# Half of the small transfers from GpSimd, two preparation steps in one slot, and a ring of seven `c` tiles in a three-network kernel on one core

## The chip, the cores and the metric

The kernel runs on one core of a Trainium2 chip. The metric is the device time of one execution in microseconds (us). The engines are TensorE (PE: matmuls, with PEld its weight loads), VectorE (DVE), ScalarE (ACT), GpSimd (POOL), and SyncE (SP), which here only issues transfers.

## The reference

Three computations in a row, all in float32:

- Linear attention with decay, for 4 batches, 8 heads, 768 positions and head size 48. For every position, `state = alpha * state + k v^T` and `y = q state`. The outputs of the heads side by side are x, 3072 tokens by 384.
- A network on x: `h = x @ w_in` (384 to 2048), ELU of h, times `w_out` (2048 to 384).
- Four experts on that result: for each expert, `relu(x @ w1) @ w2` (384 to 1024 to 384), and the sum of the four weighted by the token's probabilities, which are divided by their sum first.

## The kernel before

Every float32 operand of a matmul is split into a high part and a low part, and each product is three matmuls: high by high, high by low, low by high. So each matrix that one engine makes for PE needs a pass for the high part (mostly ACT) and one for the low part (DVE or POOL).

**Network 1** runs over 96 items: 6 chunks of 512 tokens by 16 blocks of the hidden size. An item has two halves: nine matmuls of the first layer (L618) into a bank of PSUM, and nine of the second layer (L643), which take the block of two items ago. The first items are written out by hand. From item 5 on (L1185) a table `slots` (L1059 to L1071) says which step of the attention runs in which half item: a chunk is four units (one batch, 128 positions each), and the four units of the next chunk are spread over the items of the present one. A unit has the steps prep1 (L409), prep2 (L425), scores (L431), the output (`yout_t`, L471) with the state (L513), and `xtrans` (L534), which splits the output into the two parts that network 1 reads. Work that waits for another engine is put into a queue (`later`, L130) and issued at the next `flush`.

The output of a unit is copied from PSUM to the tile `yt` by ACT (L499). Six small transfers within SBUF (L505), 16 partitions by 128 elements each, then put its heads into place; SP issues all six. `xtrans` reads `yt`: ACT makes the high part (L545), DVE the low part (L546).

**Network 2** (from 502 us) has 33 iterations: 3 groups of 1024 tokens (r) by 11 blocks of hidden units (q). The products of the first layer are not taken block by block, but by a scheme with fewer matrix products: an iteration has 15 steps, each one product of three matmuls (L922) into one of two banks h0 and h1, and DVE (L936, L938, L942; POOL where no bank takes part) adds and subtracts the results into tiles `u` and, when a hidden block is complete, into a tile `c`. Each `c` then goes through `relu` (L895): ACT writes the high part (L897) and the ReLU in place (L898), POOL the low part (L900). The second layer of the iteration before (L969) is spread between the steps. When an expert ends, six products with the probabilities are taken by DVE (`gate`, L988), each into a `c` tile as well, and added to the sum by POOL (L991), at the very end by DVE.

The inputs of the first layer are sums of blocks of x. For the groups r = 1 and 2, `prep_x` (L805) makes them during q = 1 to 8 of the group before, two in an iteration, 15 in all: POOL adds (L829), ACT makes the high part (L837) and POOL the low part (L834) of a tile `xh`, which SP sends to DRAM. The `xh` tiles come from the pool tag "g", which has three buffers.

Where a `c` lies is decided by a counter in `ctile` (L842), the number of the tile modulo 5: one buffer of the tag U6, twice the tag "e" (two buffers), once "wr", once the tag "g" of `xh`. A tile from a tag takes the buffer that comes free first in the program's order, and its first writer waits until the last reader of what lay there is done.

[...]

Of the kernel before, what the change touches and what calls it, by code (L numbers as in the profile page):

```python
# [8 lines left out]
F32 = mybir.dt.float32  # L9
# [6 lines left out]
ALU = mybir.AluOpType  # L16
AX = mybir.AxisListType

B, H, S, D = 4, 8, 768, 48
# [17 lines left out]
LISTED = 5  # L37
# [3 lines left out]
NPR = NCH // 2  # L41
NG = 11
# [26 lines left out]
STEPS2 = (  # L69
    STEPS[:7] + ((6, STEPS[7][1][::2]), STEPS[8], (3, (("+", (0, 2), "b", "S2"),)), STEPS[14])  # L70
)
# [31 lines left out]
class _Fast:  # L103
# [367 lines left out]
    def yout_t(self, u):  # L471


        nc = self.nc
        c, b = u
        raw = self.raw[u]
        ps = [self.abank(), self.abank()]

        def to(h, n):
            r, c0 = 64 * (swap(h) % 2), h // 4 * C  # L480
            return ps[h // 2 % 2][r:r + n, c0:c0 + C]

        for h in range(H):
            a, r = h // 2, slice(64 * (h % 2), 64 * (h % 2) + D)
            nc.tensor.matmul(  # L485
                to(h, 64), self.st[b][r, a, :], raw[r, Q0 + a * C:Q0 + (a + 1) * C],
                start=(a < 2), stop=False, skip_group_check=True,
            )
        for h in range(H):
            nc.tensor.matmul(  # L490
                to(h, D), raw[:, V0 + h * D:V0 + (h + 1) * D],
                self.sm[u, h % 2][:, h // 2, :], start=False, stop=True, skip_group_check=True,
            )
        del self.sm[u, 0], self.sm[u, 1]

        def pack():
            y = self.ap.tile([128, NP * C], F32, tag="y", name="yt")
            for n in range(2):
                nc.scalar.copy(  # L499
                    y[0:SW].rearrange("p (a w t) -> p w a t", w=2, t=C)[:, n],  # L500
                    ps[n][0:SW, 0:2 * C].rearrange("p (a t) -> p a t", t=C),
                )
            for j in range(2):
                for k in range(KD):
                    nc.sync.dma_start(  # L505
                        out=y[64 * j + D:64 * j + 64, k * C:(k + 1) * C],
                        in_=y[64 * j + 16 * k:64 * j + 16 * k + 16, DM:NP * C],
                    )
            self.y[u] = y[:, 0:DM].rearrange("p (k t) -> p k t", k=KD)

        self.later(pack)
# [19 lines left out]

        self.later(decay)

    def xtrans(self, u):  # L534
        nc = self.nc
        c, b = u
        v = self.y.pop(u)
        if c not in self.x0:
            self.x0[c] = self.big.tile([128, 2, KD, 512], F32R, tag=f"X{c % 2}", name=f"x0_{c % 2}")
        x0 = self.x0[c]  # L540
        self.split(x0[:, 0, :, b * C:(b + 1) * C], x0[:, 1, :, b * C:(b + 1) * C], v)

    def split(self, hi, lo, src, eng=None):
        nc = self.nc
# [296 lines left out]

    def ctile(self):  # L842
        self.cn += 1
        i = self.cn % 5
        if i == 4:
            return self.uslot(6, "c")
        if i % 2:
            return self.ep.tile([128, 512], F32, tag="e", name="c")
        if i:
            return self.wp.tile([128, 3, DM], F32, tag="wr", name="c").rearrange("p n d -> p (n d)")[:, 0:512]  # L850
        return self.hp.tile([128, 2, 512], F32, tag="g", name="c")[:, 0]

# [39 lines left out]
                )  # L892
            self.pb[r, e, m] = t

    def relu(self, g, n, v):  # L895
        nc = self.nc
        nc.scalar.activation(out=g[:, n, 0], in_=v, func=AF.Relu)  # L897
        nc.scalar.activation(out=v, in_=v, func=AF.Relu)  # L898
        self.later(
            lambda: nc.gpsimd.tensor_tensor(out=g[:, n, 1], in0=v, in1=g[:, n, 0].bitcast(F32), op=ALU.subtract)  # L900
        )

    def layer1(self, i, extra):

        nc = self.nc
        r, q = divmod(i, NG)
        wa = self.wa[i]
        S, G = {}, {}
# [4 lines left out]
        for n, (p, ops) in enumerate(STEPS if q < NG - 1 else STEPS2):  # L913
# [9 lines left out]
            for op, dst, a0, a1 in ops:  # L923
                if isinstance(dst, tuple):
                    m, f = dst
# [4 lines left out]
                    out = self.ctile()  # L930
                else:
                    if dst not in S:
                        S[dst] = self.uslot(int(dst[1]), "u")
                    out = S[dst]
                if op == "=":
                    nc.vector.tensor_copy(out, b)  # L936
                elif op == "n":
                    nc.vector.scalar_tensor_tensor(  # L938
                        out=out, in0=val(a0, b), scalar=-1.0, in1=val(a1, b), op0=ALU.mult, op1=ALU.subtract
                    )  # L940
                else:
                    (nc.vector if "b" in (a0, a1) or dst == "S5" else nc.gpsimd).tensor_tensor(  # L942
                        out=out, in0=val(a0, b), in1=val(a1, b), op=ALU.add if op == "+" else ALU.subtract
                    )
                if isinstance(dst, tuple):
                    self.relu(G[m], f, out)
            extra(n)
        return G

# [67 lines left out]
    def run(self):  # L1017
# [40 lines left out]
        slots = {}  # L1058
        for c in range(1, NCH):  # L1059
            steps = [s for u in units[4 * c:4 * c + 4] for s in seq[units.index(u)]]  # L1060
            end = F1 * c
            av = half(end - F1, end - 3)
            if c == 1:
                av = half(LISTED, end - 1)
                steps[0:5] = [steps[2]]
            for n, s in enumerate(steps):
                k = av[n * len(av) // len(steps)]
                slots.setdefault(k, []).append(s)
                if n % 6 == (1 if c == 1 else 5) and (c, n) != (1, 1):
                    slots[k].append([(load_next, ())])  # L1070
            slots.setdefault((end - 1 if c == 1 else end - 2, c != 1), []).append([(self.xtrans, ((c, B - 1),))])  # L1071

        def open_p2():
            self.attn.__exit__(None, None, None)
# [400 lines left out]
```

## Time and profile before

| | us |
|---|---|
| median of 3 runs (1238.07 to 1242.77) | 1238.5 |
| profiled execution | 1237.87 |
| its span | 1236.1 |
| PE busy | 1219.7 (99%) |
| DVE busy | 868.1 (70%) |
| ACT busy | 589.5 (48%) |
| POOL busy | 490.9 (40%) |

The span is the time from the first to the last instruction of one profiled execution; 1.8 us of that execution lie around it. Busy shares are means over stages with different loads. In the timeline a row is one instruction, or several of one line in a row (x3), and the brackets give the engine's idle time before it and who ended it. A row of PEld is the load of a matmul's weights; where PE stands, it is nearly always the load that waits, and its row names what for.

### The profile page before, as it was taken

To read this page: it belongs to the slowest core of one execution; us is meant where nothing else is said; L and a number is where in the kernel's file an instruction comes from. 1 tells how busy PE (TensorE), PEld (TensorE's weight loads), DVE (VectorE), ACT (ScalarE), POOL (GpSimd) and SP (SyncE) were. 2 spreads that over 40 slices of the span, in tenths; PEclk is the share of its full clock that TensorE was granted. 3 is DMA by queue.
4 is the path that set the end of the run, shared out by engine and by line. 5 is a ranking of instruction groups with operands and counts; after the bars stand their busy time and mean duration, and the time that the engine had idled before them with its cause. 6 is when DMAs were issued, how large, how long until landed. Compare 5 with 4: busy or idle time off the path is not lost.

```text
span 1236.1 us, 17787 instructions
## 1 busy us (share of the span) xinstructions
PE 1219.7 (99%) x6469; PEld 993.6 (80%) x6469; DVE 868.1 (70%) x1433; ACT 589.5 (48%) x1092; POOL 490.9 (40%) x388
## 2 busy tenths in 40 slices
PE   8999999999999999999999999999999999999997
PEld 5787888888887888788888887888888878888886
DVE  9995877777777678657576757675766566667664
ACT  6885566666666566434334332433433233342231
POOL 2000000000000000387688847857977474456662
PEclk9999999999999999999999999999999999999999
DMA  9632554555546467536555577763656864344331
GB/s 377 218 107 89 184 182 180 184 188 200 183 164 212 144 217 266 189 141 230 192 191 208 214 289 277 256 219 143 229 192 228 326 235 169 120 159 165 107 134 57
DMA packets 64815, 239.92 MB, mean 194 GB/s; under 512 B 7640, under 2 KB 33464, under 8 KB 55376
## 3 DMA queue, kind: packets, MB, share of 16 engines
q1 hardware_dynamic: 63856, 233.99, 53.1%
q10 hardware_dynamic: 864, 4.72, 1.0%
q8 instruction: 53, 0.87, 0.3%
q14 instruction: 42, 0.34, 0.1%
HBM read 178.27 MB, written 59.42 MB: 192 GB/s over the span
## 4 chain that ended last, share of the span: by engine, by line
PE 91%; DVE 4%; POOL 1%; issue 1%; ACT 1%; DMA 0%; SPq 0%; ACTq 0%; DVEq 0%; POOLq 0%
PE h L922 25%; PE t L643 15%; PE h L618 15%; PE t L969 15%; PE a L969 11%; PE h L969 5%; PE a L439 2%; PE a L490 2%; PE a L485 1%; PE h L460 1%; PE h L521 1%; POOL acc L991 0%; DVE s_s L263 0%; DMA raw<-in_att_dram 0%; POOL c L942 0%
## 5 line engine op out<-in xcount | busy, mean ns | idle before, releaser
L900 POOL TENSOR_TENSOR g_W<-c,g_W 128x512 fp32r<-128x512 f32 x128 | 164.7, 1297 | 627.3 <-ACT c L898 599.0
L942 DVE TENSOR_TENSOR u<-h,u 128x512 f32<-128x512 f32 x258 | 177.5, 688 | 85.9 <-PE h L922 84.6
L922 PE MATMUL h<-xc_Q,wa 128*128 128x512 f32 x780 | 218.9, 390 | 0.2 <-DVE u L942 0.2
L618 PE MATMUL h<-x,w_W 128*128 128x512 f32 x864 | 214.3, 392 | 2.5 <-DVE x L546 1.3
L643 PE MATMUL t<-g,w_W 128*128 128x512 f32 x864 | 215.4, 393 | 0.0
L897 ACT ACTIVATE g_W<-c 128x512 fp32r<-128x512 f32 x128 | 80.3, 627 | 269.7 <-DVE c L942 155.9
L618 PEld LDWEIGHTS h<-x,w_W 128*128 128x128 f32 x864 | 160.5, 188 | 37.5 <-DVE x L546 1.7
L643 PEld LDWEIGHTS t<-g,w_W 128*128 128x128 f32 x864 | 160.3, 188 | 33.9 <-issue 0.4
L922 PEld LDWEIGHTS h<-xc_Q,wa 128*128 128x128 f32 x780 | 145.9, 188 | 32.1 <-DVE u L942 1.7
L969 PE MATMUL t<-g_W,wb 128*128 128x512 f32 x576 | 157.6, 389 | 0.0
L969 PEld LDWEIGHTS t<-g_W,wb 128*128 128x128 f32 x576 | 108.1, 188 | 22.5
L898 ACT ACTIVATE c<-c 128x512 f32<-128x512 f32 x192 | 121.5, 633 | 7.4
L942 DVE TENSOR_TENSOR c<-u,h 128x512 f32<-128x512 f32 x123 | 84.3, 686 | 48.9 <-PE h L922 43.3
L629 DVE SCALAR_TENSOR_TENSOR h<-e,h 128x512 f32<-128x512 f32 x96 | 66.6, 693 | 71.8 <-ACT e L628 71.5
L922 PE MATMUL h<-xc_W,wa 128*128 128x512 f32 x390 | 109.7, 390 | 2.2 <-DVE u L942 2.2
L900 POOL TENSOR_TENSOR g_X<-c,g_X 128x512 fp32r<-128x512 f32 x64 | 82.1, 1295 | 68.0 <-ACT c L898 64.8
L936 DVE COPY u<-h 128x512 f32<-128x512 f32 x99 | 68.0, 690 | 58.0 <-PE h L922 57.7
L969 PE MATMUL a<-g_W,wb 128*128 128x512 f32 x384 | 108.2, 389 | 0.0
L897 ACT ACTIVATE g_X<-c 128x512 fp32r<-128x512 f32 x64 | 40.1, 627 | 131.5 <-DVE c L942 72.9
L922 PEld LDWEIGHTS h<-xc_W,wa 128*128 128x128 f32 x390 | 73.0, 188 | 18.2 <-DVE u L942 3.2
L627 ACT ACTIVATE e<-h 128x512 f32<-128x512 f32 x96 | 57.1, 595 | 57.8 <-PE h L618 56.4
L969 PEld LDWEIGHTS a<-g_W,wb 128*128 128x128 f32 x384 | 72.1, 188 | 15.0
(163 smaller groups left out, 1790.2 us busy)
## 6 DMA issues: line engine op xcount, KB each, us to landing
wa<-wad SPq DMA_DIRECT2D x33, 1536.0 KB, 6.6
wb<-wbd SPq DMA_DIRECT2D x30, 1536.0 KB, 7.3
raw<-in_att_dram SPq DMA_DIRECT2D x22, 964.0 KB, 5.9
wad<-wh SPq DMA_DIRECT2D x44, 384.0 KB, 2.9
wbd<-wh SPq DMA_DIRECT2D x43, 384.0 KB, 3.4
xcd<-xh SPq DMA_DIRECT2D x30, 512.0 KB, 3.5
wraw<-in_we_dram SPq DMA_DIRECT2D x20, 576.0 KB, 4.8
xc_Q<-xcd SPq DMA_DIRECT2D x6, 1536.0 KB, 7.7
```

The lines of the kernel that those rows point to most:

```text
L439: nc.tensor.matmul(ps[j][:, a * C:(a + 1) * C], raw[r, K0 + a * C:K0 + (a + 1) * C], raw[r, Q0 + a * C:Q0 + (a + 1) * C], start=True, stop ...
L618: nc.tensor.matmul(h[:, 0:n], w[:, wl, fi, k * 128:(k + 1) * 128], x[:, xl, k, n0:n0 + n], start=((k, wl, xl) == TERMS[0]), stop=((k, wl, ...
L627: nc.scalar.activation(out=e, in_=h, func=AF.Relu, scale=-1.0)
L629: return lambda: nc.vector.scalar_tensor_tensor(out=h, in0=e, scalar=-1.0, in1=h, op0=ALU.add, op1=ALU.max)
L643: nc.tensor.matmul(self.xa[k][:, 0:n], w[:, wl, fi, DM + k * 128:DM + (k + 1) * 128], g[:, gl, 0:n], start=(first and i == 0), stop=(last ...
L897: nc.scalar.activation(out=g[:, n, 0], in_=v, func=AF.Relu)
L898: nc.scalar.activation(out=v, in_=v, func=AF.Relu)
L900: lambda: nc.gpsimd.tensor_tensor(out=g[:, n, 1], in0=v, in1=g[:, n, 0].bitcast(F32), op=ALU.subtract)
L922: nc.tensor.matmul(b, w[:, wl], x[:, xl], start=(j == 0), stop=(j == 2))
L936: nc.vector.tensor_copy(out, b)
L942: (nc.vector if "b" in (a0, a1) or dst == "S5" else nc.gpsimd).tensor_tensor(out=out, in0=val(a0, b), in1=val(a1, b), op=ALU.add if op == ...
L969: nc.tensor.matmul(oa[m, d], wt[:, f, wl, d * 128:(d + 1) * 128], G[m][:, f, gl], start=first, stop=last)
```

## The change

It has four parts.

- In `pack` the transfers of the second half of the heads (j = 1) are issued by POOL; SP issues the other three.
- In chunk 1's table, prep1 and prep2 of its first prepared unit are put into one slot, so there are 19 slots where 20 were, over one half item less. The steps behind it stand earlier by up to a half item. The last `xtrans` of the chunk stays where it is, but issues its low part at once and not at the next `flush`.
- The ring of `c` tiles has seven places: U6 at remainder 3, "e" at 0 and 2, "wr" at 1, and the tag "g" at 4, 5 and 6.
- In the last iteration of network 2 the last two low parts of `relu` are computed by DVE in place of POOL.

```diff
--- before.py
+++ after.py
@@ -502,7 +502,7 @@
                 )
             for j in range(2):
                 for k in range(KD):
-                    nc.sync.dma_start(
+                    (nc.sync, nc.gpsimd)[j].dma_start(
                         out=y[64 * j + D:64 * j + 64, k * C:(k + 1) * C],
                         in_=y[64 * j + 16 * k:64 * j + 16 * k + 16, DM:NP * C],
                     )
@@ -531,7 +531,7 @@
 
         self.later(decay)
 
-    def xtrans(self, u):
+    def xtrans(self, u, now=False):
         nc = self.nc
         c, b = u
         v = self.y.pop(u)
@@ -539,6 +539,8 @@
             self.x0[c] = self.big.tile([128, 2, KD, 512], F32R, tag=f"X{c % 2}", name=f"x0_{c % 2}")
         x0 = self.x0[c]
         self.split(x0[:, 0, :, b * C:(b + 1) * C], x0[:, 1, :, b * C:(b + 1) * C], v)
+        if now:
+            self.queue.pop()()
 
     def split(self, hi, lo, src, eng=None):
         nc = self.nc
@@ -841,12 +843,12 @@
 
     def ctile(self):
         self.cn += 1
-        i = self.cn % 5
-        if i == 4:
+        i = self.cn % 7
+        if i == 3:
             return self.uslot(6, "c")
-        if i % 2:
+        if i in (0, 2):
             return self.ep.tile([128, 512], F32, tag="e", name="c")
-        if i:
+        if i == 1:
             return self.wp.tile([128, 3, DM], F32, tag="wr", name="c").rearrange("p n d -> p (n d)")[:, 0:512]
         return self.hp.tile([128, 2, 512], F32, tag="g", name="c")[:, 0]
 
@@ -892,12 +894,12 @@
                 )
             self.pb[r, e, m] = t
 
-    def relu(self, g, n, v):
+    def relu(self, g, n, v, eng):
         nc = self.nc
         nc.scalar.activation(out=g[:, n, 0], in_=v, func=AF.Relu)
         nc.scalar.activation(out=v, in_=v, func=AF.Relu)
         self.later(
-            lambda: nc.gpsimd.tensor_tensor(out=g[:, n, 1], in0=v, in1=g[:, n, 0].bitcast(F32), op=ALU.subtract)
+            lambda: eng.tensor_tensor(out=g[:, n, 1], in0=v, in1=g[:, n, 0].bitcast(F32), op=ALU.subtract)
         )
 
     def layer1(self, i, extra):
@@ -943,7 +945,7 @@
                         out=out, in0=val(a0, b), in1=val(a1, b), op=ALU.add if op == "+" else ALU.subtract
                     )
                 if isinstance(dst, tuple):
-                    self.relu(G[m], f, out)
+                    self.relu(G[m], f, out, nc.vector if i == NPR * NG - 1 and n >= len(STEPS2) - 2 else nc.gpsimd)
             extra(n)
         return G
 
@@ -1061,14 +1063,14 @@
             end = F1 * c
             av = half(end - F1, end - 3)
             if c == 1:
-                av = half(LISTED, end - 1)
-                steps[0:5] = [steps[2]]
+                av = half(LISTED, end - 1)[:-1]
+                steps[0:6] = [steps[2] + steps[5]]
             for n, s in enumerate(steps):
                 k = av[n * len(av) // len(steps)]
                 slots.setdefault(k, []).append(s)
-                if n % 6 == (1 if c == 1 else 5) and (c, n) != (1, 1):
+                if n % 6 == (0 if c == 1 else 5) and (c, n) != (1, 0):
                     slots[k].append([(load_next, ())])
-            slots.setdefault((end - 1 if c == 1 else end - 2, c != 1), []).append([(self.xtrans, ((c, B - 1),))])
+            slots.setdefault((end - 1 if c == 1 else end - 2, c != 1), []).append([(self.xtrans, ((c, B - 1), c == 1))])
 
         def open_p2():
             self.attn.__exit__(None, None, None)
```

Line numbers from L541 on are higher by two in the changed kernel. How the instructions of DVE move is seen at three places.

The first is the end of chunk 0, on DVE. L629 and L635 (L631 and L637 after) belong to the ELU of an item, L429 to a unit's prep2, and L546 (L548 after) is the low part of the last output of the chunk, which is read from `yt`. Before:

```order
L429 TENSOR_TENSOR raw<-raw,P 128x512
L635 TENSOR_TENSOR g<-h_1164,g 128x512
L629 SCALAR_TENSOR_TENSOR h_1237<-e,h_1237 128x512
L546 TENSOR_TENSOR x_1_821<-yt,x_1_821 128x3x128
L635 TENSOR_TENSOR g<-h_1237,g 128x512
L629 SCALAR_TENSOR_TENSOR h_1265<-e,h_1265 128x512
L447 TENSOR_TENSOR sm<-a_1276,mask 128x512
```

and after:

```order
L429 TENSOR_TENSOR raw<-raw,P 128x512
L637 TENSOR_TENSOR g<-h_1131,g 128x512
L631 SCALAR_TENSOR_TENSOR h_1192<-e,h_1192 128x512
L637 TENSOR_TENSOR g<-h_1192,g 128x512
L548 TENSOR_TENSOR x_1_806<-yt,x_1_806 128x3x128
L631 SCALAR_TENSOR_TENSOR h_1237<-e,h_1237 128x512
L637 TENSOR_TENSOR g<-h_1237,g 128x512
```

The low part of the output has moved ahead of the ELU's step for the block h_1237; before, it stood behind it.

The second is in network 2, on DVE, where the trace of before stands at 648 to 651 us; the number behind a name tells tiles of one name apart, and the brackets hold the engines and transfers whose semaphores the instruction waits for. Before:

```order
L942 TENSOR_TENSOR c_6466<-u_6337,h1_6460 128x512 [waits DVE_49,Pool_49]
L942 TENSOR_TENSOR c_6479<-u_6406,h0_6475 128x512 [waits DVE_49,PE_49,Pool_49]
L942 TENSOR_TENSOR u_6320<-h0_6475,u_6320 128x512 [waits Pool_49]
L942 TENSOR_TENSOR c_6494<-u_6320,h1_6490 128x512 [waits DVE_49,PE_49]
L936 COPY u_6513<-h0_6509 128x512 [waits PE_49,Pool_49]
```

and after:

```order
L944 TENSOR_TENSOR c_6466<-u_6337,h1_6460 128x512 [waits DVE_49,Pool_49]
L944 TENSOR_TENSOR c_6479<-u_6406,h0_6475 128x512 [waits DMAHW1_49,DVE_49,DMAHW5_49,PE_49,Activation_49]
L944 TENSOR_TENSOR u_6320<-h0_6475,u_6320 128x512 [waits Pool_49]
L944 TENSOR_TENSOR c_6494<-u_6320,h1_6490 128x512 [waits DVE_49,PE_49,Pool_49]
L938 COPY u_6513<-h0_6509 128x512 [waits PE_49]
```

The order is the same, but the write of c_6494 now waits for POOL too: its buffer is that of c_6466, two `c` tiles before it, which POOL's L902 reads.

The third is the end of the program, on DVE: the last two `c` tiles of network 2, and the first products with the probabilities. Before:

```order
L942 TENSOR_TENSOR u<-h_11150,u 128x512
L942 TENSOR_TENSOR c<-h_11165,u 128x512
L942 TENSOR_TENSOR c<-u,h_11179 128x512
L988 TENSOR_TENSOR c<-a_9432,pb 128x512
L991 TENSOR_TENSOR acc<-acc,c 128x512
L988 TENSOR_TENSOR c<-a_9433,pb 128x512
L991 TENSOR_TENSOR acc<-acc,c 128x512
L988 TENSOR_TENSOR c<-h_9434,pb 128x512
```

and after:

```order
L944 TENSOR_TENSOR u<-h_11150,u 128x512
L944 TENSOR_TENSOR c<-h_11165,u 128x512
L902 TENSOR_TENSOR g_W_11169<-c,g_W_11169 128x512
L944 TENSOR_TENSOR c<-u,h_11179 128x512
L902 TENSOR_TENSOR g_W_11169<-c,g_W_11169 128x512
L990 TENSOR_TENSOR c<-a_9432,pb 128x512
L993 TENSOR_TENSOR acc<-acc,c 128x512
L990 TENSOR_TENSOR c<-a_9433,pb 128x512
L993 TENSOR_TENSOR acc<-acc,c 128x512
L990 TENSOR_TENSOR c<-h_9434,pb 128x512
```

Each of the last two `c` is now followed on DVE by its low part (L902), so the second `c` and the first product stand behind a low part that needs ACT's result.

## Rows read from the trace of the kernel before

**Rows 1.** The page, part 1: busy us (share of span) xinstructions.
```profile
PE 1219.7 (99%) x6469; PEld 993.6 (80%) x6469; DVE 868.1 (70%) x1433; ACT 589.5 (48%) x1092; POOL 490.9 (40%) x388
```

**Rows 2.** Waits of PE's weight loads: line, releaser: us, times, longest.
```profile
PEld h L922 <- DVE u L942: 4.9, 9, 1.5
```

**Rows 3.** Timeline, 104 to 113 us: start, duration, engine, line [idle before <-releaser].
```profile
104.75 3.67 SPq L505 DMA_DIRECT2D yt<-yt  x6
...
109.64 0.51 ACT L545 CAST x<-yt 128x384 fp32r<-128x384 f32 x1 [4.27 <-DMA yt<-yt]
...
111.95 0.55 DVE L546 TENSOR_TENSOR x<-yt,x 128x384 fp32r<-128x384 f32 x1
...
112.56 1.69 PEld L618 LDWEIGHTS h<-x,w_W 128*128 128x128 f32 x8 [1.70 <-DVE x L546]
```

**Rows 4.** Timeline, 57 to 59 us, DVE and PE.
```profile
57.24 0.69 DVE L419 SCALAR_TENSOR_TENSOR raw<-nt,raw 128x512 f32<-128x512 f32 x1
...
58.08 2.20 PE L618 MATMUL h<-x,w_W 128*128 128x512 f32 x9
```

**Rows 5.** View of the tile yt, its DMAs.
```profile
DMA to landing us min/median/max: 1.7/2.1/7.3
```

**Rows 6.** Timeline, 755 us, DVE.
```profile
755.52 0.69 DVE L942 TENSOR_TENSOR c<-u,h 128x512 f32<-128x512 f32 x1 [1.22 <-POOL g_X L900]
```

**Rows 7.** Timeline, 649 to 651 us, DVE, PEld and POOL.
```profile
649.26 0.69 DVE L942 TENSOR_TENSOR c<-u,h 128x512 f32<-128x512 f32 x1 [0.47 <-PE h L922]
...
650.88 0.64 PEld L922 LDWEIGHTS h<-xc_Q,wa 128*128 128x128 f32 x3
...
650.95 2.55 POOL L900 TENSOR_TENSOR g_X<-c,g_X 128x512 fp32r<-128x512 f32 x2
```

**Rows 8.** Timeline, 691 to 694 us, DVE, PEld and POOL.
```profile
691.39 0.68 DVE L942 TENSOR_TENSOR c<-u,h 128x512 f32<-128x512 f32 x1
...
693.09 0.64 PEld L922 LDWEIGHTS h<-xc_W,wb 128*128 128x128 f32 x3
...
693.37 1.29 POOL L900 TENSOR_TENSOR g_X<-c,g_X 128x512 fp32r<-128x512 f32 x1
```

**Rows 9.** Timeline, 844 us, DVE and POOL.
```profile
844.30 0.69 DVE L942 TENSOR_TENSOR c<-u,h 128x512 f32<-128x512 f32 x1 [0.36 <-PE h L922]
844.49 1.32 POOL L900 TENSOR_TENSOR g_W<-c,g_W 128x512 fp32r<-128x512 f32 x1
```

**Rows 10.** Timeline, 878 to 881 us, DVE, POOL and PEld.
```profile
878.40 0.68 DVE L988 TENSOR_TENSOR c<-t,pb 128x512 f32<-128x512 f32 x1
...
879.46 1.29 POOL L991 TENSOR_TENSOR acc<-acc,c 128x512 f32<-128x512 f32 x1
...
880.76 0.64 PEld L922 LDWEIGHTS h<-xc_Q,wa 128*128 128x128 f32 x3
```

**Rows 11.** Timeline, 934 to 939 us, DVE, PEld and POOL.
```profile
934.25 0.68 DVE L942 TENSOR_TENSOR c<-u,h 128x512 f32<-128x512 f32 x1
...
936.33 0.64 PEld L922 LDWEIGHTS h<-xc_W,wa 128*128 128x128 f32 x3
...
938.77 1.31 POOL L900 TENSOR_TENSOR g_W<-c,g_W 128x512 fp32r<-128x512 f32 x1
```

**Rows 12.** Timeline, 1220 to 1225 us, ACT, POOL, DVE and PE.
```profile
1220.03 0.63 ACT L898 ACTIVATE c<-c 128x512 f32<-128x512 f32 x1
...
1220.81 2.54 POOL L900 TENSOR_TENSOR g_W<-c,g_W 128x512 fp32r<-128x512 f32 x2
...
1222.43 0.69 DVE L988 TENSOR_TENSOR c<-a,pb 128x512 f32<-128x512 f32 x1 [2.24 <-PE a L969]
...
1224.90 4.24 PE L969 MATMUL t<-g_W,wb 128*128 128x512 f32 x18
```

**Rows 13.** Windows after the last matmul: stretch, busy us of PE, PEld, DVE, ACT, POOL, PEclk.
```profile
1230.00:1232.00 2.00, 0.00 (x0) 0.00 (x0) 0.60 (x1) 0.00 (x0) 0.00 (x0) 1.00 0.64 213
1232.00:1236.00 4.00, 0.00 (x0) 0.00 (x0) 0.00 (x0) 0.00 (x0) 0.00 (x0) 0.51 0.11 37
```

## The prediction

> **What bounds the kernel now.** I read the page's part 1 first: PE is busy for 1219.7 of 1236.1 us [rows 1]. Whatever the change saves on another engine is therefore worth nothing unless PE stood for it, and whatever makes PE stand is paid whole. So the next view is what PE's weight loads waited for. It is short: in network 2 the loads of L922 wait for a DVE sum nine times, 4.9 us together and never more than 1.5 [rows 2]. The one wait in network 1 that the change aims at is read in the timeline at the end of chunk 0 [rows 3]. Last come the places in the timeline where a `c` tile is written, because there the new ring decides.
>
> PE's margin there is thin. Each step of layer 1 puts three matmuls into one of two banks (h0, h1) and DVE must empty a bank before PE may load for the next step in it. A DVE instruction that is late by more than about 0.9 us stops PE.
>
> **Transfers on two queues and the shared slot.** At the end of chunk 0 SP issues the six transfers of the last unit in 3.67 us from 104.75. ACT's L545 waits 4.27 us for them until 109.64, DVE's L546 behind it runs only at 111.95, and PE stands 1.70 us for that [rows 3]. After the change that unit's attention output stands a half item earlier, some 2.0 us (a group of nine matmuls is 2.2 with the pipeline's ends, [rows 4]); each queue issues three transfers, which saves 3 x 0.6 us; and L546 is ahead of L629 instead of behind it, as the built program shows. Each of the three alone is worth more than the stand, or nearly: I book the whole of it, −1.66 (1.70 less the pipeline's 0.04).
>
> The cost of a transfer from POOL isn't in the trace of before, as no `yt` comes from there. The nearest row is SP's: 1.7 us at best, 2.1 in the median, 7.3 at worst from issue to landing [rows 5]. POOL has no other instruction in network 1, so its issuing hides entirely. The first issue comes at 104.75 − 2.0 = 102.7, the last of three ends 1.8 later; with 2.1 us more the data are there at 106.6 and the gain stands. With 7.3 they are there at 111.8, 2.2 us later than SP's were, and the gain becomes a loss of as much as 0.6. I take 2.1, the median, because the queue carries nothing else. In the other 19 units at least five half items (10 us) lie between the output and its reader, more than either end.
>
> The price of the shared slot is at its other end. L429 of the first prepared unit now goes ahead of L635, L593 and the three instructions up to L419, so L419, which ended at 57.93 [rows 4], ends 0.6 us later, 58.54. Its reader, the scores on PE, takes the place where L618 begins at 58.08 and could load at about 58.2: +0.4 (from 0 to 0.6).
>
> **Ring of seven, what it frees.** At two iteration changes DVE stands 1.22 us because the buffer of its `c` is still read by POOL, and PE stands for it [rows 6] (the second such row is at 997). With seven buffers, the tiles written there take buffers whose readers ended more than 3 us before. Freed: 2 x 1.22 = −2.44.
>
> **Ring of seven, what it costs.** Three of the seven (numbers 4, 5, 6, one after the other) now come from the pool tag "g" with its three buffers, and `prep_x` takes its `xh` tiles from the same three. Before, it was one of five. While an `xh` holds one of the three, the third `c` can't have it and gets the buffer of the `c` two before it. That one has been written by DVE just before, and must still pass ACT (twice 0.63) and POOL's low part. So DVE waits for POOL. This happens in r = 0 and 1 only, where `prep_x` runs. In the built program I find six such pairs. For each I take the time of the write and the end of POOL's reader from the timeline of before, and give the rest of the sum at PE:
>
> - At 649.26 the write [rows 7]: POOL's reader is the first of two from 650.95, which ends at 652.23. DVE is 3.0 late, ends at 652.96, and PE's load into that bank, before at 650.88, comes at 653.0: **+2.1**. The 0.9 that is missing is PE's margin.
> - At 691.39 [rows 8]: the reader ends at 694.66, DVE is 3.3 late, the load goes from 693.09 to 695.43 (+2.34). A product with the gate's weights and two more sums stand behind it on DVE at a pitch of 0.60 and cost the next load another 0.23: **+2.6**.
> - At 844.30 [rows 9]: the reader ends at 845.81, DVE is 1.5 late; less the same margin of 0.9: **+0.6**.
> - The sixth pair, at 868, comes within the margin: **0**.
> - At 878.40 [rows 10] the gate's product must wait for POOL's sum, which ends at 880.75. Behind it on DVE is a sum `u` of the same length that empties a bank, and ends at 882.06 where PE wanted to load at 880.76: **+1.3**.
> - At 934.25 [rows 11]: here POOL is far behind, and the reader starts only at 938.77 and ends at 940.08. DVE is 5.9 late, and the `u` behind it, which empties the bank, ends at 941.40. PE's load goes from 936.33 to 941.46: **+5.1**.
>
> Sum 2.1 + 2.6 + 0.6 + 0 + 1.3 + 5.1 = +11.7. As PE, DVE and ACT are late together after each, I don't carry a delay from one to the next. Bounds: if POOL were as little late at the last place as at 844 (1.5 us), its 5.1 would be 0.6, 4.5 less in all. Upwards I see nothing but what PE pays for its clock, below.
>
> **Low part on DVE in the last iteration.** The two low parts that POOL did in a row from 1220.81 to 1223.35 [rows 12] were done before PE takes them at 1224.90; nothing is saved. But on DVE they stand in the queue. The first waits for ACT's L898, which ends at 1220.66, and runs until 1221.37. The last `c` now stands behind it, from 1221.29 to 1221.98. ACT's two passes on it (0.63 each) end at 1223.28, the second low part runs from 1223.30 to 1223.99, and only then comes the first L988, before at 1222.43, now at 1223.91: 1.48 late. Six pairs of L988 and L991 follow one after the other and set the end; a gap between two of them may take up a little: **+1.4**. The bounds are 0 (if PE's last matmuls at 1229.14, and not DVE, set the end) and 1.5.
>
> **Sum.** −1.66 + 0.4 − 2.44 + 11.7 + 1.4 = +9.4. The profiled execution took 1237.87 us, 0.6 below the median 1238.5 of the runs; 1237.87 + 9.4 = 1247.3, and with the median 1247.9. I say 1247.5.
>
> **The clock.** The last matmul of the large group ends at 1229.14 [rows 12]. The granted clock is still 1.00 from 1230 to 1232 and 0.51, thus the lower level (1.2 of 2.4 GHz) for nearly all of it, from 1232 to 1236 [rows 13]. So a stand of two us and more leaves PE at full clock, but the 5.1 us at 934 may not. The Trainium skill ("TensorE: Matmul & The Clock Gate", "HAM oscillation — how this bites in real kernels") says that an idle gap between matmul bursts sends the engine back to half its clock, and its rule is to leave no such gaps; the trace agrees at the end of the program, and no row shows a gap amid the matmuls. By rows alone: each us of matmuls at the lower level costs half a us, and if that lasts as long as the stand, 5.1 us, it costs 2.6.
>
> **Rivals.**
> 1. *The ring only frees.* If POOL reaches each reader before DVE wants the buffer, the new waits vanish and only −1.66 + 0.4 − 2.44 + 1.4 = −2.3 is left: 1236, no change. It decides if POOL's readers end less than 0.9 us after the writes. For it: POOL's 490.9 us [rows 1] lie almost all in the 735 us of network 2, so it is idle for a third of that. Against it: the rows of before, where the readers end 1.5 to 5.9 after. Chance 0.10.
> 2. *Half of it.* POOL's work on `xh` depends on SP's loads, not on DVE. When DVE and PE stand, POOL catches up, and the last places find it earlier, the one at 934 above all: by the bound above 4.5 less, 1243. Against it: in POOL's queue its pieces of `xh` stand between the low parts, which wait for ACT and so for DVE. Chance 0.14.
> 3. *The clock falls at 934*, and perhaps elsewhere: 1247.5 + 2.6 = 1250. For it: the 0.51. Against it: 5.1 us is one place only. Chance 0.20.
> 4. *POOL's transfers land late*, at 7.3 us: instead of −1.66 up to +0.6 at the end of chunk 0, 1249.8, and more if other units come late too. Chance 0.06.
>
> **How the numbers follow.** The forecast has 0.50. A change under 0.5% (6.2 us, up to 1244.7 here) can't be told from none. Slower are the forecast, rivals 3 and 4 (0.76); rivals 1 and 2 give 0.24, of which 0.21 is no change and 0.03 faster, if the freed waits were worth more. Range: down to 1241, below rival 2 with a us or two to spare, and up to 1252, rival 3 with a second fall of the clock; rival 1 lies outside.
>
> **What would show it.** In the profile after: DVE writes of `c` that wait 1.5 to 5.9 us for POOL at some 649, 691, 844, 878 and 934 us plus what has gathered before; L922's loads (two lines further down) with five waits of 0.6 to 5.1 us; no waits of 1.5 at 755 and 997; no wait for the low part of x at 112; and the last instruction on DVE about 1.4 us further from the last matmul. It is wrong if DVE's waits for POOL in network 2 sum to less than 5 us, or if PE's stands are mostly elsewhere, such as behind transfers of POOL.

## The result, and the profile after

The changed kernel takes 1254.18 us (median of 6 runs, 1252.51 to 1255.06), the one before 1238.34 (6 runs in the same place): a ratio of 1.0116, with a 95% interval of 1.0097 to 1.0135. It is slower by 15.8 us. Executions of one kernel spread by some 5 us, most of it from the first 25 us, where in some of them the clock falls (the last section shows it); medians contain that, and steps inside a trace, behind those 25 us, don't. The forecast was slower by 9.2, 1247.5, and its range ended at 1252.0. The profiled execution took 1253.6 us with this page (span, and part 1):

```profile
span 1251.6 us, 17868 instructions
...
PE 1223.5 (98%) x6466; PEld 994.7 (79%) x6469; DVE 867.6 (69%) x1435; ACT 590.0 (47%) x1092; POOL 516.9 (41%) x446
```

All engines but POOL do the work they did before [rows 1]; PE's busy time is 3.8 us longer and its span 15.5, so most of the loss is time in which PE stands. Its weight loads' waits (line, releaser: us, times, longest):

```profile
PEld h L924 <- DVE u L944: 9.6, 12, 5.1
...
PEld h L924 <- DVE c L944: 4.5, 2, 2.3
```

L924 was L922: 4.9 us of waits for DVE [rows 2] have become 14.1, the longest 5.1 where it had been 1.5. DVE in its turn waits in network 2 for POOL, 17.9 us in six waits:

```profile
DVE c L944 <- POOL g_W L902: 9.0, 3, 5.7
DVE c L944 <- POOL g_X L902: 6.6, 2, 3.5
DVE c L990 <- POOL acc L993: 2.3, 1, 2.3
```

In the trace of before it was 5.2 us in six waits, none over 1.2:

```profile
DVE c L942 <- POOL g_W L900: 2.0, 2, 1.2
DVE c L988 <- POOL acc L991: 2.0, 3, 1.1
...
DVE c L942 <- POOL g_X L900: 1.2, 1, 1.2
```

These are the places of the forecast. PE's loads behind the writes that [rows 7] to [rows 11] show are now, in the same order (start, duration, engine, line, and in brackets the stand, that is how long the load waited, and its cause):

```profile
652.72 0.53 PEld L924 LDWEIGHTS h<-xc_Q,wa 128*128 128x128 f32 x3 [2.17 <-DVE c L944]
```

```profile
697.09 0.53 PEld L924 LDWEIGHTS h<-xc_W,wb 128*128 128x128 f32 x3 [2.32 <-DVE c L944]
```

```profile
851.50 0.53 PEld L924 LDWEIGHTS h<-xc_W,wa 128*128 128x128 f32 x3 [0.67 <-DVE u L944]
```

```profile
887.04 0.53 PEld L924 LDWEIGHTS h<-xc_Q,wa 128*128 128x128 f32 x3 [1.38 <-DVE u L944]
```

and at the last one, with POOL's reader and DVE's two instructions before the load:

```profile
944.94 1.26 POOL L902 TENSOR_TENSOR g_W<-c,g_W 128x512 fp32r<-128x512 f32 x1
...
946.23 0.69 DVE L944 TENSOR_TENSOR c<-u,h 128x512 f32<-128x512 f32 x1 [5.72 <-POOL g_W L902]
946.84 0.68 DVE L944 TENSOR_TENSOR u<-h,u 128x512 f32<-128x512 f32 x1
...
947.57 0.93 PEld L924 LDWEIGHTS h<-xc_W,wa 128*128 128x128 f32 x3 [5.10 <-DVE u L944]
```

POOL's reader ends at 946.20, DVE's write begins at 946.23 after 5.72 us, and the sum behind it frees PE's bank at 947.5. Behind this load there is a second loss. In the windows (stretch, busy us of PE, PEld, DVE, ACT, POOL, then PEclk, the granted clock as a share of 2.4 GHz) PE works all the time from 948 on, but until 952 it gets 6 matmuls into 2 us in place of 10:

```profile
944.00:946.00 2.00, 0.00 (x0) 0.00 (x0) 0.00 (x0) 0.00 (x0) 2.00 (x2) 0.80 1.00 412
946.00:948.00 2.00, 0.42 (x1) 0.43 (x2) 1.66 (x3) 0.95 (x2) 1.42 (x2) 0.50 0.94 379
948.00:950.00 2.00, 2.00 (x6) 1.52 (x6) 1.60 (x3) 1.57 (x3) 1.57 (x2) 0.50 1.02 375
950.00:952.00 2.00, 2.00 (x6) 1.53 (x5) 0.60 (x1) 0.00 (x0) 2.00 (x2) 0.50 0.95 350
952.00:954.00 2.00, 2.00 (x10) 1.64 (x9) 1.31 (x3) 0.00 (x0) 0.23 (x1) 0.99 1.04 436
```

The clock fell while PE stood, from 1.00 to 0.50, which is 1.2 GHz, and stayed there until 952.

The whole difference, place by place, is the start of the same weight load in the two traces (both run the same loads in the same order in network 2), PE's lag there, and what the lag gained since the place above:

| place | before | after | lag | step | forecast |
|---|---|---|---|---|---|
| first 10 us | 9.43 | 10.07 | 0.6 | +0.6 | 0 |
| before the second chunk | 79.90 | 81.16 | 1.3 | +0.6 | +0.4 |
| end of chunk 0 | 112.56 | 112.16 | −0.4 | −1.7 | −1.7 |
| `c` write at 649 | 650.88 | 652.72 | 1.8 | +2.2 | +2.1 |
| `c` write at 691 | 694.67 | 698.89 | 4.2 | +2.4 | +2.6 |
| freed wait at 755 | 756.87 | 759.69 | 2.8 | −1.4 | −1.2 |
| input of `xh` | 781.48 | 785.90 | 4.4 | +1.6 | 0 |
| `c` write at 844 | 846.54 | 851.50 | 5.0 | +0.5 | +0.6 |
| `c` write at 878 | 880.76 | 887.04 | 6.3 | +1.3 | +1.3 |
| `c` write at 934 | 936.33 | 947.57 | 11.2 | +5.0 | +5.1 |
| lower clock behind it | 939.05 | 952.26 | 13.2 | +2.0 | 0 |
| freed wait at 997 | 998.47 | 1010.46 | 12.0 | −1.2 | −1.2 |
| last group of loads | 1224.68 | 1236.88 | 12.2 | +0.2 | 0 |
| last DVE instruction, end | 1230.59 | 1244.28 | 13.7 | +1.5 | +1.4 |
| end of the span | 1236.1 | 1251.6 | 15.5 | +1.8 | 0 |

Every place that was forecast is there, with its size to 0.2 us. Four steps were not in the sum: 1.6 at 781, 2.0 of clock, 1.8 after the last instruction, and 0.8 at the start: the 0.6 of the first row, and 0.2 of the second row's 0.6, for at 50 us PE's lag is already 0.8.

The end, after: two low parts on DVE, the first product, PE's last loads, and DVE's last instruction:

```profile
1232.98 0.69 DVE L902 TENSOR_TENSOR g_W<-c,g_W 128x512 fp32r<-128x512 f32 x1 [2.17 <-ACT c L900]
...
1235.63 0.69 DVE L902 TENSOR_TENSOR g_W<-c,g_W 128x512 fp32r<-128x512 f32 x1 [1.36 <-ACT c L900]
...
1236.24 0.68 DVE L990 TENSOR_TENSOR c<-a,pb 128x512 f32<-128x512 f32 x1
1236.88 4.04 PEld L971 LDWEIGHTS t<-g_W,wb 128*128 128x128 f32 x18
...
1243.59 0.69 DVE L993 TENSOR_TENSOR acc<-acc,c 128x512 f32<-128x512 f32 x1
```

and of before the rows that answer to the last two:

```profile
1224.68 4.04 PEld L969 LDWEIGHTS t<-g_W,wb 128*128 128x128 f32 x18
...
1229.90 0.69 DVE L991 TENSOR_TENSOR acc<-acc,c 128x512 f32<-128x512 f32 x1
```

From the start of the last loads to DVE's end it was 5.91 us and is now 7.40. From DVE's end to the end of the span it was 5.5 (1236.1 − 1230.59) and is 7.3.

### The profile page after: what moved, and what is told of

It reads as the page before. It is cut to its first block, busy times and chain, and to the rows that moved or that the text cites. A ratio compares the mean times of both kernels' runs of the same rounds, so it can differ in the third digit from the quotient of the medians.

```text
span 1251.6 us, 17868 instructions
## 1 busy us (share of the span) xinstructions
PE 1223.5 (98%) x6466; PEld 994.7 (79%) x6469; DVE 867.6 (69%) x1435; ACT 590.0 (47%) x1092; POOL 516.9 (41%) x446
## 4 chain that ended last, share of the span: by engine, by line
PE 82%; POOL 7%; DVE 5%; ACT 2%; issue 2%; DMA 1%; SPq 0%; ACTq 0%; POOLq 0%; DVEq 0%
PE h L924 22%; PE t L645 15%; PE h L620 15%; PE t L971 12%; PE a L971 9%; PE h L971 4%; POOL acc L993 2%; PE a L439 2%; PE a L490 2%; POOL g_W L902 2%; PE a L485 1%; POOL xh L831 1%; DMA xraw<-x1d 1%; PE h L460 1%; POOL c L944 1%
## 5 line engine op out<-in xcount | busy, mean ns | idle before, releaser
L902 POOL TENSOR_TENSOR g_W<-c,g_W 128x512 fp32r<-128x512 f32 x126 | 162.3, 1300 | 233.7 <-ACT c L900 180.6
L924 PE MATMUL h<-xc_Q,wa 128*128 128x512 f32 x780 | 219.4, 390 | 2.9 <-DVE c L944 1.7
L505 POOL DMA_DIRECT2D yt<-yt x60 | 28.9, 488 | 370.1 <-DVE h L631 110.6
L924 PEld LDWEIGHTS h<-xc_Q,wa 128*128 128x128 f32 x780 | 145.7, 188 | 35.8 <-DVE u L944 3.5
L924 PE MATMUL h<-xc_W,wa 128*128 128x512 f32 x390 | 111.1, 394 | 4.9 <-DVE u L944 4.9
L631 DVE SCALAR_TENSOR_TENSOR h<-e,h 128x512 f32<-128x512 f32 x96 | 66.6, 693 | 69.7 <-ACT e L630 69.5
L902 POOL TENSOR_TENSOR g_X<-c,g_X 128x512 fp32r<-128x512 f32 x64 | 82.1, 1295 | 72.9 <-ACT c L900 48.4
L924 PEld LDWEIGHTS h<-xc_W,wa 128*128 128x128 f32 x390 | 73.7, 190 | 21.4 <-DVE u L944 6.2
L629 ACT ACTIVATE e<-h 128x512 f32<-128x512 f32 x96 | 57.3, 597 | 62.2 <-PE h L620 60.9
```

What stands on the lines that cost most here:

```text
L505: (nc.sync, nc.gpsimd)[j].dma_start(out=y[64 * j + D:64 * j + 64, k * C:(k + 1) * C], in_=y[64 * j + 16 * k:64 * j + 16 * k + 16, DM:NP * C],)
L629: nc.scalar.activation(out=e, in_=h, func=AF.Relu, scale=-1.0)
L631: return lambda: nc.vector.scalar_tensor_tensor(out=h, in0=e, scalar=-1.0, in1=h, op0=ALU.add, op1=ALU.max)
L902: lambda: eng.tensor_tensor(out=g[:, n, 1], in0=v, in1=g[:, n, 0].bitcast(F32), op=ALU.subtract)
L924: nc.tensor.matmul(b, w[:, wl], x[:, xl], start=(j == 0), stop=(j == 2))
```

## The experiments

Each was run beside the kernel before, whose runs lie between 1237.6 and 1243.2 us. Steps are read inside the traces, against the profile of before.

**The ring alone (ring_only, ring_only_2).**

```diff
-        i = self.cn % 5
-        if i == 4:
+        i = self.cn % 7
+        if i == 3:
             return self.uslot(6, "c")
-        if i % 2:
+        if i in (0, 2):
...
-        if i:
+        if i == 1:
```

> The kernel before with the ring of seven alone. Theory (the ring's new waits): the same places in network 2 as in the trace after, so PE is later by 2.2 + 2.4 + 0.6 + 1.3 + 5.0 at the five writes, 2.0 by the lower clock behind the last, 2.6 less at the two freed waits and 1.6 more for what comes back near 780 us: about +12.5 us, 1251. Rival (the transfers from POOL are the main cause): no more than my blind sum for the ring, +9.3, or less, with POOL's descriptors out of the way.

> The kernel with the ring of seven alone once more, for a second profile: the first began 4.7 us later in its first 20 us than the profile of before. Theory: whatever the start does, the steps at the five places in network 2 are 2.1, 2.2, 0.5, 1.3 and 5.0 again, and the clock falls behind the last for about 2 us of loss. Rival: they vary by more than 0.5 us from one execution to the next, and the clock behind the last wait with them.

Measured: 1254.62 us (5 runs, 1252.89 to 1255.16), ratio 1.0115 [1.0094, 1.0136]; the second time 1251.3 (2 runs), ratio 1.0101 [1.0083, 1.0119]. The start differs: the first profile is 4.7 us behind at 80 us, the second 0.0. Without it PE's lag at the last loads is 11.9 and 14.1 us. The steps at the five writes are 2.1, 2.2, 0.5, 1.3, 5.0 both times. The freed waits give 1.4 and 1.3 us at 755 and 1.1 and 0.8 at 997, and 1.0 and 1.2 come back at 781. All instructions of PE, DVE, ACT and POOL stand in the second trace in the order of before; only the waits differ. So the ring makes the loss that the changed kernel shows in network 2, alone. What varies most is the clock. Behind the last stand it costs 2.3 and 2.6 us, and in the second profile it fell also behind the stand at 691 us (row, and the window that follows; 6 matmuls in 2 us):

```profile
697.37 0.53 PEld L922 LDWEIGHTS h<-xc_W,wb 128*128 128x128 f32 x3 [2.31 <-DVE c L942]
```

```profile
699.00:701.00 2.00, 2.00 (x6) 1.49 (x5) 1.40 (x3) 1.94 (x4) 2.00 (x3) 0.50 0.93 373
```

PE's lag grows by 1.5 in the 5 us from this load on, by 0.2 in the first profile and in that of the changed kernel, for the same stand. So the five steps repeat to 0.1 us, and the clock does not.

**The three other parts without the ring (no_ring).** The changed kernel with `ctile` of before.

> The changed kernel with the ring of five of before; the other three parts stay. Theory: what is left of the loss is the end of the program (1.8), the low parts on DVE (1.5), and the gain of 1.1 to 1.6 at the end of chunk 0: about +2, 1240. Rival (the parts hurt each other, so the ring alone isn't the cause): 1245 or more.

Measured: 1241.01 us (12 runs), ratio 1.0025 [1.0015, 1.0035], some 2.7 us slower. In its trace the step at the end of chunk 0 is −1.7, DVE's end is 1.4 further from the last load, and the end of the span 2.3 further from DVE. The parts add up: 2.7 here and 13.0 of the ring alone (the second time, 1251.3 beside 1238.3) are 15.7, and the changed kernel loses 15.8.

**Each of the other parts alone (slots_only, relu_only, dma_only).** Each is the diff's part of that name on the kernel before.

> The kernel before with the shared slot and the early low part alone, all transfers on SP. Theory: PE's wait of 1.7 us at 112 us goes through the half item and the order on DVE without POOL's help: -1.5 there, +0.4 at the scores near 58 us, -1.1 in all, 1237.2. Rival (the six issues in a row on SP are what is late): the wait keeps half of its length or more, and the time is 1238 or above.

Measured: 1237.43 (12 runs), ratio 0.9985 [0.9971, 0.9999]. The step at 112 us is −1.7: the shared slot, and the low part ahead of the ELU's step, take the whole wait away with all six transfers on SP. The slot's price at the scores is 0.4 (PE's lag is 4.05 at 55 us and 4.46 at 60).

> The kernel before with the last two low parts on DVE alone. Theory: the last DVE instruction stands 1.4 to 1.5 us further from the last matmul, and the time is 1.5 above, 1239.8. Rival (the end is set by the outputs' transfers, which overlap): no change, 1238.3.

Measured: 1240.33 (12 runs), ratio 1.0015 [1.0003, 1.0028], 1.6 slower. From the last loads to DVE's end it takes 7.34 us for 5.91. From there to the end of the span it is 5.6, for 5.5 before.

> The kernel before with half of the small transfers on POOL and nothing else. Theory: the end of the program is 1.8 us longer, because the closing waits after the last output count more semaphores and stand once for 1.5 us; at the end of chunk 0 PE's wait of 1.7 goes or shrinks: between 0 and +1.8 in all. Rival (transfers from POOL delay other things too): +4 us or more, with new waits of PE in network 1. Second rival: the 1.8 us at the end belong to the layout of the program and not to these transfers, then -1.5 or 0.

Measured: 1239.31 (12 runs), ratio 1.0002 [0.9991, 1.0012]. PE gains 1.0 of the 1.7 at the end of chunk 0. In its trace the last DVE instruction and the span are

```profile
1231.65 0.69 DVE L991 TENSOR_TENSOR acc<-acc,c 128x512 f32<-128x512 f32 x1
```

```profile
span 1239.6 us, 17897 instructions
```

that is 7.2 us after DVE's end (1232.34; the span to two digits is 1239.55), where before has 5.5. The gain is given back. From POOL's first transfer at 52 us on, PE's lag grows nowhere in network 1.

**How many transfers (dma_one, dma_one_b, dma_eight).**

```diff
-                    nc.sync.dma_start(
+                    (nc.gpsimd if j and k == 0 and u[0] in (1, 2) else nc.sync).dma_start(
```

(dma_eight; dma_one_b has `u == (1, 3)`; in dma_one the unit was (0, 3), which another code path handles, so that kernel issued what the kernel before does, and its result says nothing of POOL's transfers.)

> The kernel before with one of the 120 small transfers on POOL (one of the last unit of chunk 0), all others on SP. Theory (the longer end of the program comes with POOL's having a queue of its own at all): the end after the last output is 1.8 us longer or nearly so, 1240.0. Rival (it comes with their number): no change at the end, 1238.3.

> The kernel before with one of the 120 small transfers on POOL (one of the last unit before the second chunk's items begin), all others on SP; in dma_one the unit chosen wasn't one that this line issues, so no transfer had moved. Theory (the end is longer because the closing waits count one more semaphore for each that POOL's transfers use): the time from the last DVE instruction to the end of the span is 5.5 to 5.8 us, as before or a little more. Rival (the longer end comes with POOL's queue being used at all): 7.2 us or more.

> As dma_one_b with eight transfers on POOL, one of each of eight units, so that all eight semaphores of POOL's transfers are in use. Theory (the number of semaphores): 7.2 us or more from the last DVE instruction to the end, as with sixty. Rival (the number of transfers): 5.5 to 6.2.

Measured: dma_one 1240.44 (10 runs), ratio 1.0006 [0.9996, 1.0017], a second measure of the kernel before, with the same end of 5.5 us. dma_one_b 1240.59 (1 run): 5.7 us from DVE's end to the span's. dma_eight 1238.51 (1 run):

```profile
1229.92 0.69 DVE L991 TENSOR_TENSOR acc<-acc,c 128x512 f32<-128x512 f32 x1
```

```profile
span 1236.5 us, 17830 instructions
```

5.9 us. The kernels without transfers from POOL have 5.4 to 5.6. So my theory is wrong: one transfer costs 0.1, eight, with which all eight semaphores of POOL's transfers are in use, cost 0.4, and sixty cost 1.7 to 2.3. That fits their number, with one execution each of one and of eight; but the eight also end earlier, at 186 us where the sixty end at 424, and no run parts the two. In the traces with sixty the SP engine stands once for 1.4 to 1.7 us amid its closing semaphore events, in those with eight or fewer never over 0.5 (the first of these events comes some 3 us behind the issue of the last output in every trace). It stands in front of events that wait for semaphores of POOL's transfers, but the last of these transfers had landed some 800 us before. What it waits for the traces don't show, and this stays open.

Outside the span there is a small part more: the executions of kernels with eight or sixty transfers from POOL are 2.0 to 2.2 us longer than their spans, all others 1.7 to 1.9.

**Two long stands made on purpose (stand10, stand6).**

```diff
-                    nc.vector.tensor_copy(out, b)
+                    for _ in range(10 if (i, n) == (19, 0) else 1):
+                        nc.vector.tensor_copy(out, b)
```

> The kernel before, with one DVE copy out of a bank made ten times at one place in network 2 (iteration 19, step 0), the result the same. PE should stand there once for about 5 us and nowhere else. Theory (the clock falls in a stand of 5 us amid the matmuls, and costs 2 us more): PE is later by 5 at the place and by some 2 more in the 5 us that follow, and the granted clock shows 0.5 there. Rival (the lower clock in the changed kernel had another cause): 5 and no more, clock 1.00.

> The kernel before, with the copy out of the bank made six times in place of ten at the same place. PE should stand for about 2.8 us. Theory (a stand of this length can already bring the clock down, as the one of 2.2 us at 691 us did in one of three profiles of the ring of seven): after the stand up to 1.5 us more are lost at a granted clock of 0.5, or nothing, if it goes one way here. Rival (only stands near 5 us do it): 2.8 and no more.

Measured: stand10 1246.17 us (1 run). DVE's copies (ten times the one, and one more), and PE's load behind them:

```profile
915.26 7.81 DVE L937 COPY u<-h 128x512 f32<-128x512 f32 x11 [0.91 <-PE h L922]
...
922.53 0.93 PEld L922 LDWEIGHTS h<-xc_W,wa 128*128 128x128 f32 x3 [5.76 <-DVE u L937]
```

and the windows at and after the stand:

```profile
920.00:922.00 2.00, 0.00 (x0) 0.00 (x0) 1.90 (x4) 0.62 (x1) 0.92 (x1) 0.74 0.94 387
922.00:924.00 2.00, 1.47 (x4) 1.18 (x5) 1.67 (x3) 0.00 (x0) 0.00 (x0) 0.50 0.29 123
```

PE's lag grows by 5.7 there and by another 2.3 until 928, at 6 matmuls in 2 us. In stand6, 1245.15 us (1 run), PE is 2.8 us later than before at the place and loses another 1.5:

```profile
924.00:926.00 2.00, 2.00 (x6) 1.59 (x5) 1.24 (x2) 0.33 (x1) 0.04 (x1) 0.50 0.53 221
```

So both theories hold: each of these stands costs its length and then 1.5 to 2.3 us at half clock. The profile of dma_only has such a stand by chance, before POOL's first transfer: at 40.4 us a load of L618 waits 2.8 us for DVE, the clock falls to 0.50, and PE's lag grows by 1.6 behind it. In the kernel before no stand in network 2 is over 1.5 [rows 2], and the clock is 1.00 throughout it.

**A ring of six (ring6_only), and with the slot (slots_ring6).**

```diff
-        i = self.cn % 5
-        if i == 4:
+        i = self.cn % 6
+        if i == 3:
             return self.uslot(6, "c")
-        if i % 2:
+        if i in (0, 4):
...
-        if i:
+        if i == 1:
```

> The kernel before with a ring of six: the places of `c` modulo 6 are g, wr, g, U6, e, e (remainder 2, 1, 5, 3, 0 and 4), so two of six come from the pool tag g and never one after the other. Theory (the loss of the ring of seven is the three in a row beside an xh tile): none of the five long waits is there, the two waits of DVE for POOL at 755 and 997 us are gone, and the time is between that of before and 2.4 us less; if the freed time at 755 comes back at 780 as in the changed kernel, 1.0 to 1.3 less. Rival (any longer ring makes DVE wait for POOL, because each c is held until POOL has read it): 3 us slower or more.

Measured: 1238.51 (12 runs), ratio 1.0002 [0.9992, 1.0011]. None of the five waits is there, nor the two of 1.5 us, but a new one, for POOL's low part:

```profile
PEld h L922 <- DVE u L942: 2.3, 9, 0.6
...
PEld a L969 <- POOL g_W L900: 1.3, 1, 1.3
```

Its steps are −1.3 at 755, +1.3 at 781 and −1.3 at 997. The time is not less, though 1.0 to 1.3 less was expected: the medians contain the spread of the start. In the trace PE's lag goes from 0.4 at 112 us to −0.8 at the last loads. So a longer ring as such doesn't make DVE wait: with two places of the tag of `xh` that never follow one another the five waits are gone. Whether it is that the three stand in a row, or that they are three, no run parts; the reuse of a buffer after two tiles, seen in the order of DVE's instructions, speaks for the first. And the freed wait at 755 comes back.

> The kernel before with the shared slot (and the early low part) and the ring of six, no transfers from POOL and no low parts on DVE. Theory (the parts add up): 1.1 less by the slot, 1.2 less by the ring of six: 1236.0, faster than both kernels. Rival (the two gains are one, or the noise of the start hides them): 1237.5 or above.

Measured: 1238.04 (11 runs, 1235.22 to 1240.37), ratio 0.9985 [0.9973, 0.9996]. The steps in its trace are those of the two parts, −1.7 at the end of chunk 0 and −1.4 in all behind it. The median is higher than forecast: in 7 of 11 runs the mean clock is 0.996 or less, as in the profiled one, where it fell in the first 25 us. The four others have 1235.2 to 1236.4, around the forecast of 1236.0.

**Where the freed wait goes (early_raw).** The same, and `prep_x` of the third group begins one iteration earlier with its load.

```diff
-                if q == 1:
+                if q == 1 - r:
                     xs = self.prep_x(r + 1)
+                    if r:
+                        put(2, do, xs[0])
...
-                        put(2 + 7 * n, do, s)
+                        if (r, q, n) != (1, 1, 0):
+                            put(2 + 7 * n, do, s)
```

> The kernel of slots_ring6, and for the third group of tokens the raw blocks of x (xraw) are loaded one iteration earlier, ahead of the outputs of the first group in SP's queue. Theory (the freed wait at 755 us comes back at 781 because POOL's input of xh, loaded behind the outputs that wait for POOL, is no earlier than before): PE's step of +1.2 at 781 us is gone and the time is 1.2 less than slots_ring6, 1234.8. Rival (the step at 781 has another cause, such as POOL's own load): the step stays, same time as slots_ring6.

Measured: 1235.22 (11 runs, 1234.23 to 1237.85), ratio 0.9973 [0.9962, 0.9983]. The step at 781 is gone, and PE ends 3.5 us ahead of before. The waits of L924 in network 2:

```profile
PEld h L924 <- DVE u L944: 2.3, 9, 0.6
```

They are nine as before [rows 2], but 2.3 us in place of 4.9 and none over 0.6. This is the fastest kernel of the study, 3.4 us below the one before.

## Why the prediction was wrong

**What bounds, and the ring's cost: right.** PE's margin of some 0.9 us behind a DVE write, the end of POOL's reader as the time of release, and the six pairs of tiles carried the sum: 11.7 forecast, 11.4 measured (2.2 + 2.4 + 0.5 + 1.3 + 5.0). The ring is the cause of this loss, by ring_only and no_ring.

**The clock: the step that failed most.** I had it as a rival at 0.20 with 2.6 us, with the argument that one place of 5.1 us is little, and the sum had nothing for it. The measured price is 2.0 there, 2.3 and 2.6 in the two profiles of the ring alone; stand10 shows 2.3 for a stand like it and stand6 1.5 for a shorter one. In [rows 12, 13] the last matmul ends at 1229.14, and the clock is 1.00 until 1232 and then 0.51; a stand of 5.1 us was longer than that, so its price belonged in the sum and not among the rivals. And my reading that a stand of two us and more leaves PE at full clock does not hold: ring_only_2 lost the clock in one of 2.3. The rule of the Trainium skill that I had beside it ("TensorE: Matmul & The Clock Gate", "HAM oscillation — how this bites in real kernels") now has rows amid the matmuls that agree.

**What the ring frees: half of it was no gain.** I took −2.44 at full. PE gains 1.4 at 755, but 25 us later it stands for a low part on POOL that is late by as much. The rows show why, of the kernel after:

```profile
767.07 1.32 POOL L993 TENSOR_TENSOR acc<-acc,c 128x512 f32<-128x512 f32 x1
...
769.35 5.19 SPq L755 DMA_DIRECT2D xraw<-x1d  x4
...
781.95 2.67 POOL L831 TENSOR_TENSOR xh<-xh,xraw 128x512 f32<-128x512 f32 x2 [0.91 <-DMA xraw<-x1d]
...
784.57 1.28 POOL L902 TENSOR_TENSOR g_W<-c,g_W 128x512 fp32r<-128x512 f32 x1
...
785.90 0.19 PEld L971 LDWEIGHTS a<-g_W,wb 128*128 128x128 f32 x1 [1.32 <-POOL g_W L902]
```

and of the one before:

```profile
762.93 1.30 POOL L991 TENSOR_TENSOR acc<-acc,c 128x512 f32<-128x512 f32 x1
...
765.73 3.33 SPq L753 DMA_DIRECT2D xraw<-x1d  x4
...
777.26 2.66 POOL L829 TENSOR_TENSOR xh<-xh,xraw 128x512 f32<-128x512 f32 x2 [0.74 <-DMA xraw<-x1d]
...
779.87 1.31 POOL L900 TENSOR_TENSOR g_W<-c,g_W 128x512 fp32r<-128x512 f32 x1
```

At 781 the second addition of an `xh` waits for its raw data, and the low part that PE wants stands behind it in POOL's queue. SP loads those data behind the outputs of the group before, and these wait for POOL's sums (`acc`). POOL ran on at its own pace when DVE and PE gained 1.4: its last sum there is 4.1 us later than before, while PE is 2.8 later. SP's loads start 3.6 us later and end 5.5 later. early_raw loads them ahead of the outputs, and the loss is gone. I priced the stall that goes, and not what is late next.

**Transfers from POOL: landing within its bounds, end missed.** Their landing was the price that I bounded. It is that of SP's beside them (kind, size, median us from issue to landing), and for both it is longer than the 2.1 that I took:

```profile
yt<-yt SPq DMA_DIRECT2D x60, 8.0 KB, 3.1
yt<-yt POOLq DMA_DIRECT2D x60, 8.0 KB, 3.0
```

The gain at the end of chunk 0 is −1.7 as forecast, but slots_only has it without POOL, and the transfers alone bring 1.0 (dma_only): they are not worth the whole stand by themselves, as I had said of each of the three causes. What I hadn't priced at all is the end of the program: 1.8 us, which these transfers alone bring (dma_only 1.7). The trace of before has no transfer from POOL, and I bounded the unknown queue only where data are waited for, not where the program closes.

**The shared slot: right.** The scores wait for L419, which ends at 59.36, and PE's lag goes from 0.83 at 55 us to 1.26 at 64: 0.4, as forecast, and 0.4 in each of the four other kernels with the shared slot:

```profile
58.67 0.69 DVE L419 SCALAR_TENSOR_TENSOR raw<-nt,raw 128x512 f32<-128x512 f32 x1
...
59.42 0.97 PEld L439 LDWEIGHTS a<-raw 48*128 48x128 f32 x16 [0.78 <-DVE raw L419]
```

**The low parts on DVE: right**, 1.5 for 1.4 (relu_only: 1.4).

**The sum.** 9.4 forecast, 15.5 measured in the span. The places of the forecast give 9.1; 2.0 of clock, 1.6 given back at 781, 1.8 at the end, and 0.8 of the start, which differs from one execution to the next, give 6.2, and 0.2 stays without a name. So three terms that the sum had at nothing carried the time out of the range, which left room for one of them at a time.

## What to carry to other kernels

Before a pool is shared by two kinds of tiles, count how many buffers are free while the other kind holds one, and where the ring comes back to the same buffer; more places in a ring can mean a shorter distance between two uses of a buffer. Price a stand of PE amid its matmuls as its length plus what the clock takes afterwards, here 1.5 to 2.6 us for stands of 2.8 us and more. And follow a freed wait on the engines that didn't gain by it: a queue that keeps its old pace, here POOL and the loads behind it, takes the gain back at the next place where it is needed.

## What was not expected of the hardware

- In all 16 profiles together, up to the last matmul, the granted clock falls only behind a stand of a weight load (its wait, as in the brackets). Behind all stands of up to 2.0 us it stayed at 1.00. Of six stands from 2.15 to 2.32, all with the ring of seven, one was followed by a fall (ring_only_2 at 691 us, at a cost of 1.3 us). All eight from 2.37 to 2.96 were, and all four from 5.1 to 5.8.
- Six of those eight stands are at the start, where a load of L256 waits for DVE: 0.4 us in the profile of before, 2.0 or less in all ten profiles whose clock stays at 1.00 in the first 25 us, and 2.4 to 3.0 in the six whose clock falls there. With the stand itself this costs 3 to 5 us, which is most of the spread between executions. Of the first profile of ring_only, the row and a window behind it:

```profile
10.85 1.25 PEld L256 LDWEIGHTS a<-raw 48*128 48x128 f32 x16 [2.85 <-DVE raw L234]
```

```profile
12.00:16.00 4.00, 3.33 (x32) 2.61 (x32) 3.97 (x8) 0.83 (x2) 0.00 (x0) 0.50 1.01 420
```

- Sixty transfers on POOL's queue lengthen the end of the program by 1.7 to 2.3 us, eight by 0.4, in one execution with eight.
